# Attention logits turned by DMA instead of TensorE, with a new order of loads and new costs in the planner

## The chip, the core and the metric

The kernel runs on one core of a Trainium2 chip. A core has five engines, each with its own queue of instructions that it works off in order: TensorE (PE; its weight loads are PEld), VectorE (DVE), ScalarE (ACT), GpSimd (POOL) and SyncE (SP). SP computes nothing here; it issues DMAs, which ACT and POOL do as well. The metric is the device time in microseconds (us) of one execution; lower is better. A profile is taken of one execution; its span runs from the first to the last instruction of the program.

## The reference

A layer norm feeds two branches whose outputs are added to the input. Branch A is a dilated sliding-window attention: each position looks at W=8 earlier positions, 2 apart, with 32 heads of 20 elements. Branch B is a gated unit without an activation.

```
xn = layernorm(x)                        # x: 2048 x 640, bfloat16
q, k, v = xn @ wqkv                      # 32 heads of 20
logits[h,s,w] = q[h,s] . k[h, s - 2w] / sqrt(20)     # -1e9 where s - 2w < 0
attn = softmax(logits, over w)           # 8 values
o[h,s] = sum_w attn[h,s,w] * v[h, s - 2w]
out = x + o @ wo + ((xn @ w_gate) * (xn @ w_up)) @ w_down     # inner width 1536
```

## The kernel before

The 2048 rows are 16 tiles of 128 (numbered 0 to 15), in four chunks of four tiles (chunk 0 to 3). PE turns the normed rows (`x`) of the first eight tiles into `xnT`; a transposing DMA on SP does it for the other eight. From `xnT` PE makes q, k (line 338), v (line 362) and the gate and up values (line 515). The loop over chunks is `attention(c)`, `glu(c)`, then `down` for the four tiles of the chunk, in between which the layer norm of chunk c+2 is done, then q, k and v of chunk c+2.

**Attention.** For each window place i of 8, DVE multiplies q by the shifted k (`pw`, line 394; five buffers). PE sums each head's 20 products with a matrix of ones, four places at a time (line 404): a logits group. There are two groups in a chunk, numbered here 0 to 7 over the kernel. ACT copies each group from PSUM to `L` in f32 (line 413); in chunk 0 DVE then adds the mask to the first 14 columns (line 415). PE transposes `L` back, four 128x128 blocks for each half chunk (two tiles), into PSUM (`pS`, line 426). DVE takes the maximum over the window with a reduce (line 434) and subtracts it (436), ACT takes the exponential (441), DVE sums with a reduce (448), inverts (449) and multiplies (451). These last three are called the norm here.

The v rows are stored to a DRAM scratch `vD`, and SP loads each tile's eight shifted copies back into one of three `v8` buffers: "value t" is that load for tile t, 1,280 KB (line 461). DVE multiplies it by the weights (line 476) and adds the eight copies in three steps (485, 489, 491); a transposing DMA on SP turns the result into `oT` (line 498).

**glu(c)** is 24 matmul groups of five (12 gate and up pairs). ACT copies each from PSUM (line 520; three gate and two up buffers) and DVE multiplies each pair into one of the twelve `hT` (line 531). **down** accumulates twelve `hT` products (553) and five `oT` products (556) for each half of a tile, and DVE adds the rows of x to it (`xr`, line 562). For the first tile of a chunk both halves first run ten `hT` products and the five `oT` products; the last two `hT` products of both halves come after, here the closing matmuls.

**PSUM.** Six banks (`ps`) go round in turn for all of PE's main work, one holds the logits, one the transposed logits.

**What sets the order.** The program is a list of `Step`s, each with an engine, a cost, an occupancy and its dependencies. `Plan.order` runs a list schedule with them and emits the instructions in that order; nothing is reordered later, and the waits between engines follow from the tiles. Steps marked urgent go ahead of others that are ready. `floor` is the earliest end that the planner assumes for a load. PE's main work is one fixed chain; what the planner decides is between which of its pieces the logits groups fall, and how DVE's, ACT's and SP's steps interleave. On SP the early loads are chained by hand: the first x tile, the weights wv, wq, wk, gate and up, then value 0, 1, 2, then w_down (wd) and wo.

Of the kernel before, what the change touches and what calls it, by code (L numbers as in the profile page):

```python
# [9 lines left out]
ACT = mybir.ActivationFunctionType  # L10
# [4 lines left out]
class Step:  # L15


    __slots__ = ("eng", "cost", "deps", "fn", "late", "succ", "idx", "start", "end", "left", "occ", "urgent", "after", "floor")

    def __init__(self, eng, cost, fn, deps, occ=None, after=()):  # L20
        self.eng, self.cost, self.fn = eng, cost, fn
        self.after = [d for d in after if d is not None]
        self.deps = [d for d in deps if d is not None] + self.after
        self.occ = cost if occ is None else occ
        self.succ = []
        self.urgent = False
        self.floor = 0.0


class Plan:  # L30


    LAG = {"PE": 0.25, "ACT": 0.22, "DVE": 0.12, "POOL": 0.2, "SP": 0.1}
# [10 lines left out]
    def order(self):  # L44
# [15 lines left out]
        while True:  # L60
# [16 lines left out]
            for t in s.succ:  # L77
                t.left -= 1
                if t.left == 0:
                    at = max(  # L80
                        d.start + d.occ if d in t.after else d.end + (0.0 if d.eng == t.eng else self.LAG[d.eng])
# [8 lines left out]
def kernel(  # L90
# [49 lines left out]
    ident_f = const.tile([P, P], F32, name="ident_f")  # L140
# [40 lines left out]
    WL["g"].floor, WL["u"].floor = 19.0, 25.0  # L181
# [7 lines left out]

    def consts_f():  # L190
        make_identity(nc, ident_f[:])
# [28 lines left out]
    C0 = add("POOL", 1.5, consts0)  # L220
    CE = add("POOL", 1.4, consts_e, [C0])
    CM = add("POOL", 0.8, consts_m, [C0])
    CF = add("POOL", 0.7, consts_f, [C0])
# [39 lines left out]
    def ln(t):  # L263
        a = add("DVE", 0.45, ln_stats(t, 0), [X[t], GL.get(t - 3)])
        a = add("DVE", 0.45, ln_stats(t, 1), [a])
        a = GL[t] = add("DVE", 0.36, ln_aggr(t), [a])
        b = add("POOL", 0.6, ln_rstd(t), [a])
        XT[t] = add("DVE", 0.45, ln_apply(t), [b])
# [4 lines left out]
    def pe_main(cost, fn, deps=(), banks=1):  # L273
# [5 lines left out]
        main = add("PE", cost, fn, [main, *waits, *deps])  # L279
# [5 lines left out]
    def transposes(t):  # L285
# [19 lines left out]
        if t < XDMA:  # L305
            a = pe_main(0.29, pe, [XT[t]])
            TT[t] = add("ACT", 0.7, ev, [a])
            ring.append(TT[t])
        else:
            a = TT[t] = add("SP", 3.5, dma, [XT[t], GP.get(c - 2)], occ=1.0)  # L310
# [19 lines left out]
    def qk(c, lo, n, rs=(0, 1)):  # L330
        for r in rs:
            for j in range(KT):
# [14 lines left out]
                a = pe_main(KT * (n / 2400 + 0.003), pe,  # L347
                            [WK if r else WQ, *[TT[c * CH + t] for t in range(lo // P, (lo + n) // P)], LASTPW.get(c - 2)])
                e = add("ACT", 0.16 + n / 1200, ev, [a, HALOCP[c]])
# [5 lines left out]
    def vproj(t):  # L355
        c, q = divmod(t, CH)
        evs = []
        for n in range(2):
# [15 lines left out]
            e = add("ACT", 0.6, ev, [a, VS.get(t - 3), CZ])  # L374
# [6 lines left out]
        VS[t] = add("POOL", 2.2, st, evs, occ=0.5)  # L381


    PW, LL, LE, SS, DD, AA, O16, OE, V8, DT = {}, {}, {}, {}, {}, {}, {}, {}, {}, {}

    def prodlog(c):
        for g in range(2):
            n = 2 * c + g
            for j in range(4):
# [7 lines left out]
                PW[m] = add("DVE", 1.48, mul, [*Q[c], *Kk[c], LL.get((m - 5) // 4) if m >= 5 else None])  # L397
            LASTPW[c] = PW[m]

            def lg(g=g):  # L400
                l = new(("lps", c, g), [P, 512], F32, "pl", 1, psum)
# [6 lines left out]
            LL[n] = add("PE", 1.25, lg, [*[PW[8 * c + 4 * g + j] for j in range(4)], LE.get(n - 1), CE])  # L408
            LL[n].urgent = True

            def ev(g=g):
                L = new(("L", c, g), [P, CS], F32, "L", 2)
                nc.scalar.copy(L[:], T["lps", c, g][:])
                if c == 0:
                    nc.vector.tensor_tensor(L[:, 0:HALO], L[:, 0:HALO], negm[:, g, :], ALU.add)

            LE[n] = add("ACT", 0.7, ev, [LL[n], SS.get(2 * c - 1), CM])

    def softmax(c, hf):
        n = 2 * c + hf  # L420

        def tr():
            ps = new(("atp", n), [P, 2, 2, P], F32, "pS", 1, psum)
            for t in range(2):
                for g in range(2):
                    nc.tensor.transpose(ps[:, t, g, :], T["L", c, g][:, (2 * hf + t) * P : (2 * hf + t + 1) * P], ident_f[:])  # L426

        SS[n] = add("PE", 0.45, tr, [LE[2 * c], LE[2 * c + 1], DD.get(n - 1), CF])
        SS[n].urgent = True

        def mx():
            L4 = T["atp", n][:].rearrange("p t g (w h) -> p t (g w) h", w=4, h=H)
            m = sb.tile([P, 2, H], F32, name="m", tag="m", bufs=2)
            nc.vector.reduce_max(m[:], L4.rearrange("p t w h -> p t h w"), AX.X)
            d = new(("d", n), [P, 2, W, H], F32, "d", 2)
            nc.vector.tensor_tensor(d[:], L4, m[:, :, None, :].to_broadcast([P, 2, W, H]), ALU.subtract)

        DD[n] = add("DVE", 1.4, mx, [SS[n], AA.get(n - 2)])
# [4 lines left out]
        e = add("ACT", 0.65, ex, [DD[n]])  # L443

        def nrm():
            d = T["d", n]
            s = sb.tile([P, 2, H], F32, name="s", tag="s", bufs=2)
            nc.vector.reduce_sum(s[:], d[:].rearrange("p t w h -> p t h w"), AX.X)
            nc.vector.reciprocal(s[:], s[:])
            a = new(("a", n), [P, 2, W, H], BF, "a", 2)  # L450
            nc.vector.tensor_tensor(a[:], d[:], s[:, :, None, :].to_broadcast([P, 2, W, H]), ALU.mult)

        AA[n] = add("DVE", 2.2, nrm, [e, O16.get(2 * n - 3)])

    def load_v8(t):
# [6 lines left out]
        V8[t] = add("SP", 6.0, fn, [VS[t], VS.get(t - 1), O16.get(t - 3), CZ], occ=0.5, after=[WL["u"]])  # L462
        if t < 3:
            V8[t].floor = 30.0 + 4.3 * t
        if t == 2:
            WL["d"] = add("SP", 8, wload(wd, B_w_down), after=[V8[2]], occ=0.5)
            WL["o"] = add("SP", 8, wo_load, after=[WL["d"]], occ=2.0)
            WL["d"].floor, WL["o"].floor = 46.0, 49.0
# [200 lines left out]
```

## Time and profile before

| | |
|---|---|
| median of three runs (lowest, highest) | 274.73 us (272.54, 275.71) |
| the profiled execution: its time | 273.97 us |
| its span | 272.3 us |
| TensorE clock granted, mean | 0.994 |
| share of DMA engines' time, queue of SP | 43.7% |

The profile's page gives each engine's busy time, the chain of work that ended last (followed back from the last instruction to whatever released it), the costliest groups of instructions, and the DMA issues with the time until they landed. Groups read: line, engine, operation, output<-inputs, shapes, xcount | busy us in all, mean ns of one | idle time of the engine just before them, and what ended it. A timeline row reads: start us, duration us, engine, line, operation, tiles. In the rows of the chain the columns are start us, duration us, what.

The profiled execution lies within the three runs, 0.76 us under their median.

### The profile page before, as it was taken

How to read it: one execution, taken by the hardware profiler on the slowest of the kernel's cores; microseconds unless marked ns; L12 is line 12 of the kernel's file. 1: busy time of each engine (PE TensorE's matmuls, PEld its weight loads, DVE VectorE, ACT ScalarE, POOL GpSimd, SP SyncE). 2: the span in 40 equal slices, each digit the busy share in tenths (PEclk: the TensorE clock that was granted, in tenths of full speed). 3: DMA queues.
4: the chain of work that ended last, by engine and by line, in shares of the span. 5: the costliest groups of instructions: out<-in, count | busy, mean ns of one | idle time of the engine just before them, and what ended most of it. 6: DMA issues, size and time to landing. Idle time of an engine off the chain costs nothing.

```text
span 272.3 us, 4126 instructions
## 1 busy us (share of the span) xinstructions
PE 263.3 (97%) x1608; PEld 146.1 (54%) x1626; DVE 216.5 (80%) x302; ACT 108.0 (40%) x197; POOL 39.7 (15%) x83
## 2 busy tenths in 40 slices
PE   5899999999999999999999999999999999999994
PEld 1554447444476555544456664644447774445773
DVE  4644999999998968999998389999974999991221
ACT  2467656555500155465520025755551005554000
POOL 6431006400000242300001201200000212000000
PEclk9799999999999999999999999999999999999999
DMA  7999999452759830557795213697500156111001
GB/s 230 382 403 382 367 365 250 156 173 63 225 108 275 270 98 26 134 182 217 224 269 64 72 51 88 236 280 220 191 0 2 48 149 202 38 24 26 24 24 48
DMA packets 43156, 44.85 MB, mean 165 GB/s; under 512 B 17587, under 2 KB 40385, under 8 KB 43137
## 3 DMA queue, kind: packets, MB, share of 16 engines
q1 hardware_dynamic: 39168, 35.07, 43.7%
q0 software_dynamic: 2240, 7.56, 8.3%
q10 hardware_dynamic: 1728, 1.97, 2.1%
q8 instruction: 12, 0.20, 0.3%
q14 instruction: 8, 0.06, 0.1%
HBM read 35.39 MB, written 5.26 MB: 149 GB/s over the span
## 4 chain that ended last, share of the span: by engine, by line
PE 92%; DMA 4%; DVE 2%; issue 1%; ACT 0%
PE ps L515 38%; PE ps L553 19%; PE ps L338 13%; PE ps L362 8%; PE ps L556 8%; DMA x<-in_A_x_dram 4%; PE pl L404 4%; PE pS L426 1%; DVE st L238 1%; PE ps L295 1%; DVE x L257 0%; ACT xnT L299 0%; DVE mv L244 0%; DVE xr L562 0%; DVE ve L246 0%
## 5 line engine op out<-in xcount | busy, mean ns | idle before, releaser
L515 PE MATMUL ps<-xnT,wu 128*128 128x512 bf16 x240 | 59.6, 379 | 0.0
L515 PE MATMUL ps<-xnT,wg 128*128 128x512 bf16 x228 | 59.0, 379 | 0.6
L553 PE MATMUL ps<-wd,hT 128*128 128x320 bf16 x384 | 57.4, 299 | 0.0
L394 DVE TENSOR_TENSOR pw<-q,k 128x2560 bf16<-128x2560 bf16 x32 | 46.6, 1484 | 0.8 <-PE pl L404 0.7
L553 PEld LDWEIGHTS <-hT 128*128 128x128 bf16 x384 | 37.2, 98 | 16.2 <-issue 1.7
L476 DVE TENSOR_TENSOR v<-v,a 128x5120 bf16<-128x5120 bf16 x16 | 45.1, 2819 | 0.1
L515 PEld LDWEIGHTS <-wu 128*128 128x128 bf16 x240 | 23.5, 98 | 28.3
L515 PEld LDWEIGHTS <-wg 128*128 128x128 bf16 x240 | 23.4, 98 | 27.9 <-issue 0.4
L520 ACT CAST us<-ps 128x512 bf16<-128x512 f32 x48 | 28.1, 586 | 23.9 <-PE ps L515 20.3
L520 ACT CAST gs<-ps 128x512 bf16<-128x512 f32 x48 | 28.1, 586 | 20.7 <-PE ps L515 20.7
L562 DVE TENSOR_TENSOR xr<-ps,xr 128x320 bf16<-128x320 f32 x32 | 15.2, 487 | 20.7 <-PE ps L556 17.3
L584 POOL DMA_DIRECT2D out_dram<-xr x14 | 7.6, 542 | 139.7 <-DVE xr L562 139.3
L556 PE MATMUL ps<-wo,oT 128*128 128x320 bf16 x160 | 27.0, 299 | 0.0
L531 DVE TENSOR_TENSOR hT<-gs,us 128x512 bf16<-128x512 bf16 x48 | 19.7, 420 | 8.9 <-ACT us L520 8.8
L362 PE MATMUL ps<-wv,xnT 128*128 128x320 bf16 x160 | 24.2, 308 | 0.3 <-ACT xnT L299 0.3
L485 DVE TENSOR_TENSOR v<-v 128x2560 bf16<-128x2560 bf16 x16 | 23.7, 1484 | 0.1
L338 PE MATMUL ps<-xnT,wq 128*128 128x512 bf16 x96 | 22.4, 379 | 0.2
L238 DVE BATCH_NORM_STATS2 st<-x 128x6 f32<-128x320 bf16 x32 | 14.0, 482 | 10.3 <-DMA x<-in_A_x_dram 10.1
L338 PE MATMUL ps<-xnT,wk 128*128 128x512 bf16 x98 | 22.0, 379 | 0.1
L362 PEld LDWEIGHTS <-xnT 128*128 128x128 bf16 x160 | 15.8, 100 | 7.5 <-ACT xnT L299 0.5
L345 ACT CAST q<-ps 128x512 bf16<-128x512 f32 x20 | 11.7, 585 | 18.3 <-PE ps L338 17.3
L556 PEld LDWEIGHTS <-oT 128*128 128x128 bf16 x160 | 15.7, 98 | 6.1
(51 smaller groups left out, 191.6 us busy)
## 6 DMA issues: line engine op xcount, KB each, us to landing
v<-vD SPq DMA_DIRECT2D x16, 1280.0 KB, 7.3
vD<-v_t POOLq DMA_DIRECT2D x16, 160.0 KB, 2.7
xr<-in_A_x_dram POOLq DMA_DIRECT2D x16, 160.0 KB, 2.6
out_dram<-xr POOLq DMA_DIRECT2D x14, 160.0 KB, 2.1
x<-in_A_x_dram ACTq DMA_DIRECT2D x12, 160.0 KB, 6.1
wg<-in_B_w_gate_dram SPq DMA_DIRECT2D x1, 1920.0 KB, 14.7
wu<-in_B_w_up_dram SPq DMA_DIRECT2D x1, 1920.0 KB, 18.8
wd<-in_B_w_down_dram SPq DMA_DIRECT2D x1, 1920.0 KB, 19.9
```

Of the source, the lines that this page charges most:

```text
L238: nc.vector.bn_stats(T["st", t][:, g, :], T["x", t][:, g * NS : (g + 1) * NS])
L338: nc.tensor.matmul(ps[:, 0:n], lhsT=(wk if r else wq)[:, i, j * P : (j + 1) * P], rhs=T["xnT", c][:, i, lo : lo + n], start=(i == 0), stop ...
L362: nc.tensor.matmul(ps[:, 0:NS], lhsT=T["xnT", c][:, i, q * P : (q + 1) * P], rhs=wv[:, i, n * NS : (n + 1) * NS], start=(i == 0), stop=(i ...
L394: nc.vector.tensor_tensor(p[:], T["q", c][:], T["k", c][:, :, DIL * i : DIL * i + CS], ALU.mult)
L476: nc.vector.tensor_tensor(v[:].rearrange("p w (j h) -> p w j h", j=Dh, h=H), v[:].rearrange("p w (j h) -> p w j h", j=Dh, h=H), T["a", n][ ...
L485: nc.vector.tensor_tensor(v[:, 0:4, :], v[:, 0:4, :], v[:, 4:8, :], ALU.add)
L515: nc.tensor.matmul(ps[:], lhsT=(wu if r else wg)[:, i, f * P : (f + 1) * P], rhs=T["xnT", c][:, i, :], start=(i == 0), stop=(i == KT - 1))
L520: nc.scalar.copy(s[:], T[key][:])
L531: nc.vector.tensor_tensor(h[:], T["gs", c, f][:], T["us", c, f][:], ALU.mult)
L553: nc.tensor.matmul(ps[:, 0:NS], lhsT=T["hT", c, f][:, q * P : (q + 1) * P], rhs=wd[:, f, sl], start=(f == 0), stop=(f == FT - 1 and not wo ...
L556: nc.tensor.matmul(ps[:, 0:NS], lhsT=T["oT", t][:, g, :], rhs=wo[:, g, sl], start=False, stop=(g == KT - 1 and f1 == FT))
L562: nc.vector.tensor_tensor(T["xr", t][:, sl], T["psD", t, n][:, 0:NS], T["xr", t][:, sl], ALU.add)
```

## The change

Logits. The copy on ACT now writes `L` in bf16; the mask of chunk 0 is added by DVE in PSUM before that copy. A transposing DMA on SP turns each group into `LT`, one bf16 buffer for the whole chunk; a chunk's softmax needs both groups. The eight sets of f32 transposes on PE are gone, and with them the f32 identity that POOL made. The freed PSUM bank gives the logits two. The two reduces become three pairwise steps each over the window (8 to 4 to 2 to 1): bf16 for the maximum, f32 for the sum.

SP's early loads now go value 0, wd, logits 0, value 1, logits 1, wo, value 2.

The planner has new costs: for steps of DVE, PE and ACT that follow each other on one engine only the occupancy counts, the lag between engines is 0.06, logits groups are held back by a margin of 0.5 after their products, and the floors of loads are new.

The diff, without most of the lines that only change a cost:

```diff
-    LAG = {"PE": 0.25, "ACT": 0.22, "DVE": 0.12, "POOL": 0.2, "SP": 0.1}
+    LAG = 0.06
+    INORDER = ("DVE", "PE", "ACT")
...
-                        d.start + d.occ if d in t.after else d.end + (0.0 if d.eng == t.eng else self.LAG[d.eng])
+                        d.start + d.occ if d in t.after else (d.start + d.occ if d.eng == t.eng and d.eng in self.INORDER else d.end + (0.0 if d.eng == t.eng else self.LAG) + t.margin)
...
-    WL["g"].floor, WL["u"].floor = 19.0, 25.0
+    WV.floor, WQ.floor, WK.floor = 6.4, 13.6, 13.7
+    WL["g"].floor, WL["u"].floor = 18.0, 25.2
...
-    CF = add("POOL", 0.7, consts_f, [C0])
...
-                l = new(("lps", c, g), [P, 512], F32, "pl", 1, psum)
+                l = new(("lps", c, g), [P, 512], F32, "pl", 2, psum)
...
-            LL[n] = add("PE", 1.25, lg, [*[PW[8 * c + 4 * g + j] for j in range(4)], LE.get(n - 1), CE])
+            LL[n] = add("PE", 1.28, lg, [*[PW[8 * c + 4 * g + j] for j in range(4)], LE.get(n - 2), CE], occ=1.195)
             LL[n].urgent = True
+            LL[n].margin = 0.5
 
             def ev(g=g):
-                L = new(("L", c, g), [P, CS], F32, "L", 2)
+                L = new(("L", c, g), [P, CS], BF, "L", 2)
+                if c == 0:
+                    ps = T["lps", c, g]
+                    nc.vector.tensor_tensor(ps[:, 0:HALO], ps[:, 0:HALO], negm[:, g, :], ALU.add)
                 nc.scalar.copy(L[:], T["lps", c, g][:])
-                if c == 0:
-                    nc.vector.tensor_tensor(L[:, 0:HALO], L[:, 0:HALO], negm[:, g, :], ALU.add)
...
+            def tr(g=g):
+                if g == 0:
+                    new(("LT", c), [P, CH, W, H], BF, "LT", 1)
+                out = T["LT", c][:].rearrange("p t (g w) h -> p t g (w h)", g=2)[:, :, g, :]
+                nc.sync.dma_start_transpose(out=out, in_=T["L", c, g][:])
+
+            early = [SPLAST[0]] if c == 0 else []
+            SS[n] = SPLAST[0] = add("SP", 3.5, tr, [LE[n], DD.get(2 * c - 1), DD.get(2 * c - 2)], occ=1.25, after=early)
+            if c == 0 and g == 0:
+                load_v8(1)
+                SPLAST[0] = V8[1]
...
-        def tr():
-            ps = new(("atp", n), [P, 2, 2, P], F32, "pS", 1, psum)
-            for t in range(2):
-                for g in range(2):
-                    nc.tensor.transpose(ps[:, t, g, :], T["L", c, g][:, (2 * hf + t) * P : (2 * hf + t + 1) * P], ident_f[:])
...
-            nc.vector.reduce_max(m[:], L4.rearrange("p t w h -> p t h w"), AX.X)
+            nc.vector.tensor_tensor(m[:], L4[:, :, 0:4, :], L4[:, :, 4:8, :], ALU.max)
+            nc.vector.tensor_tensor(m[:, :, 0:2, :], m[:, :, 0:2, :], m[:, :, 2:4, :], ALU.max)
+            nc.vector.tensor_tensor(m[:, :, 0:1, :], m[:, :, 0:1, :], m[:, :, 1:2, :], ALU.max)
...
-            nc.vector.reduce_sum(s[:], d[:].rearrange("p t w h -> p t h w"), AX.X)
-            nc.vector.reciprocal(s[:], s[:])
+            nc.vector.tensor_tensor(s[:], d[:, :, 0:4, :], d[:, :, 4:8, :], ALU.add)
+            nc.vector.tensor_tensor(s[:, :, 0:2, :], s[:, :, 0:2, :], s[:, :, 2:4, :], ALU.add)
+            nc.vector.tensor_tensor(s[:, :, 0:1, :], s[:, :, 0:1, :], s[:, :, 1:2, :], ALU.add)
+            nc.vector.reciprocal(s[:, :, 0, :], s[:, :, 0, :])
...
+    def load_down():
+        WL["d"] = SPLAST[0] = add("SP", 8, wload(wd, B_w_down), after=[SPLAST[0]], occ=0.5)
+        WL["d"].floor = 36.0
+
+    def load_out():
+        WL["o"] = SPLAST[0] = add("SP", 8, wo_load, after=[SPLAST[0]], occ=5.0)
+        WL["o"].floor = 49.0
...
     def attention(c):
+        if c == 0:
+            SPLAST[0] = WL["u"]
+            load_v8(0)
+            load_down()
         prodlog(c)
+        if c == 0:
+            load_out()
+            load_v8(2)
```

In the changed program, as built, PE's main chain is the same. The logits groups move along it: group 2 from behind tile 2 of down(0) to behind tile 1, group 3 from behind the first q group of chunk 2 into the middle of tile 3 of down(0), group 4 from behind the first products of tile 0 of down(1) to behind the eleventh pair of glu(1), group 5 to where group 4 was, groups 6 and 7 from behind 18 and 24 matmul groups of glu(2) to behind 11 and 16. On DVE, three products of chunk 1 stand ahead of the first softmax (before: one), and both halves' maxima stand together ahead of the first norm. In chunk 1 the order on SP is `oT` of tile 3, values 5 and 6, the x tiles 13, 14 and 15, logits 2 and 3; before it was value 5, x tiles 13 and 14, `oT` of tile 3, value 6, x tile 15.

## The prediction

> **What bounds the kernel now.** First the busy times, then the chain of waits, then the groups that the change touches.
>
> ```profile
> PE 263.3 (97%) x1608; PEld 146.1 (54%) x1626; DVE 216.5 (80%) x302; ACT 108.0 (40%) x197; POOL 39.7 (15%) x83
> ...
> PE 92%; DMA 4%; DVE 2%; issue 1%; ACT 0%
> PE ps L515 38%; PE ps L553 19%; PE ps L338 13%; PE ps L362 8%; PE ps L556 8%; DMA x<-in_A_x_dram 4%; PE pl L404 4%; PE pS L426 1%; DVE st L238 1%; PE ps L295 1%; DVE x L257 0%; ACT xnT L299 0%; DVE mv L244 0%; DVE xr L562 0%; DVE ve L246 0%
> ```
>
> PE is the bound, and the transposes to be removed (L426) are on its chain. But DVE's 80% is no even 80%: it is over 95% busy from 40 to 80 us, so it is the second bound there. The groups, kept apart by shape:
>
> ```profile
> L531 DVE TENSOR_TENSOR hT<-gs,us 128x512 bf16<-128x512 bf16 x48 | 19.7, 420 | 8.9 <-ACT us L520 8.8
> L448 DVE TENSOR_REDUCE s<-d 128x64 f32<-128x512 f32 x8 | 8.3, 1032 | 0.7 <-ACT d L441 0.7
> L451 DVE TENSOR_TENSOR a<-d,s 128x512 bf16<-128x512 f32 x8 | 5.5, 692 | 0.3
> L436 DVE TENSOR_TENSOR d<-pS,m 128x512 f32<-128x512 f32 x8 | 5.5, 692 | 0.3
> L434 DVE TENSOR_REDUCE m<-pS 128x64 f32<-128x512 f32 x8 | 5.5, 686 | 3.6 <-PE pS L426 3.6
> L426 PE MATMUL pS<-ident_f,L 128*128 128x128 f32 x32 | 4.8, 272 | 0.0
> L449 DVE RECIPROCAL s<-s 128x64 f32<-128x64 f32 x8 | 4.4, 553 | 0.3
> ```
>
> Then the timelines of PE and DVE, the chain between 73 and 90 us, SP's issues, and two stretches of the traffic (the last number is GB/s):
>
> ```profile
> 41.91 1.53 PE L362 MATMUL ps<-wv,xnT 128*128 128x320 bf16 x10
> 43.28 0.60 PE L426 MATMUL pS<-ident_f,L 128*128 128x128 f32 x4
> 43.71 2.88 PE L362 MATMUL ps<-wv,xnT 128*128 128x320 bf16 x20
> ```
> ```profile
> 49.21 2.82 DVE L476 TENSOR_TENSOR v<-v,a 128x5120 bf16<-128x5120 bf16 x1
> ...
> 75.86 0.42 DVE L531 TENSOR_TENSOR hT<-gs,us 128x512 bf16<-128x512 bf16 x1
> ```
> ```profile
> 78.36 2.17 PE ps L553 x16
> ```
> ```profile
> 79.62 0.53 SPq L461 DMA_DIRECT2D v<-vD  x1
> ...
> 83.59 4.36 SPq L159 DMA_DIRECT2D x<-in_A_x_dram  x1
> ```
> ```profile
> 86.50:88.50 2.00, 2.00 (x21) 1.19 (x22) 1.98 (x3) 0.00 (x0) 0.04 (x1) 1.00 1.42 131
> 89.00:93.00 4.00, 4.00 (x36) 2.71 (x29) 3.93 (x7) 0.58 (x1) 0.55 (x1) 1.00 1.10 366
> ```
> ```profile
> 94.50 2.44 DVE L238 BATCH_NORM_STATS2 st<-x 128x6 f32<-128x320 bf16 x6
> ```
>
> DVE finishes the twelfth hT of chunk 0 at 76.3; PE's closing matmuls, which start at 78.36, need it at 78.5. DVE has 2.2 us to spare.
>
> **Off PE.** Ten value matmuls take 1.36 on the chain, but the next twenty start 1.80 after the first ten (41.91 to 43.71): one set of four transposes costs 0.44. Eight sets: 3.5 us, each on the path.
>
> **Start.** Tile 0 is normed ahead of the second half of tile 2's statistics, one piece of 0.4, so PE starts 0.4 sooner. Group 1 needs the eighth product, though. The products start about 0.3 sooner, with the k copies and x tile 9; then three pieces of statistics stand before the mask instead of two (+0.4). So the eighth still ends at 40.4, and group 1 starts at 40.5 instead of 40.78. Gain 0.3 (0, if x tile 9 is no earlier, to 0.8).
>
> **DVE's new steps.** Pairwise bf16 work has rows at 512 (420 ns) and 2560 elements (1484): 0.15 + 0.52 per thousand, so the maxima over 256, 128 and 64 take 0.29, 0.22, 0.19; the subtraction stays 0.69. In f32 (692 at 512, same fixed part) the sums take 0.42, 0.29, 0.22. A step that needs the one before it starts 0.035 after it; an independent one 0.08 before its end. So the maximum and subtraction take 1.41, the norm 2.23. Before, start to start, 1.33 (58.69 to 60.02) and 2.26 (62.39 to 64.65). Nothing gained; the order is what matters.
>
> **Chunk 0: hT 12 (a new wait).** From 40.4 DVE has two statistics 0.80, three aggregates 0.90, a product 1.42, the mask 0.10, three rows normed 1.08, two more products 2.83: 47.5. The transposed logits must be there: mask done 43.7, copy 0.585, so issued at 44.35; the transposing DMA of five blocks lands in 2.6, here four, 47.0. Hidden, by 0.5. Then two maxima 2.82, norm 2.23: 52.6 (before: 49.21). Up to hT 12: eleven hT 3.69, four value multiplies 10.96, three first adds 4.34, three second adds 3.78, the second norm 2.23: 77.6, done 78.05. The same rows over the old order give 75.5 against 75.86, 0.4 of it waits. PE needs it at 78.5 - 0.28 - 0.88 = 77.35. Stall 0.7. Bounds: 0, if dependent steps overlap like the others; 2.4, if that DMA takes the slowest `xnT` transpose's 4.3 (+1.2) and the maxima run at the f32 price (+0.5). Group 2 then finds its products ready within 0.1: both engines are late by the same amount.
>
> A rule speaks against moving this work. The Trainium skill, VectorE: DVE Perf Modes, section The three transpose paths, gives 390 ns for a 128x128 transpose on TensorE and 1309 ns for one by DMA, and its rules say to use TensorE if PSUM will do. The trace is cheaper: five blocks land in 2.6. By the page's price, an estimate, four blocks take 5.2 us, the logits land at 49.6 and the stall grows by 2.1; the sum below would be +1.0 instead of -1.1.
>
> **Chunk 1: group 4 (the other new wait).** It moves forward into glu(1), to where PE arrives at 112.72 - 1.76 - 0.28 + 0.7 = 111.4, plus eleven pairs at 2.137 (24 groups took 112.72 to 138.36): 134.9. Its fourth product is DVE's last thing after all of chunk 1's attention. That starts after x tile 15: before, it landed at 94.54 and DVE's six statistics began then. Now SP gets to value 5 later: chunk 0's last result at 80.8, its transpose, 82.1. Value 5, value 6 and three x tiles, 3.1 MB, are queued ahead of tile 15's landing and of logits 2 and 3. At best one value lands in its shortest 5.4 and the other 1.8 MB moves at 350 GB/s (338 and 366 in the two clean stretches of this traffic), 5.1: 92.6. At worst the 14.9 of before (79.62 to 94.54): 97.0. With the median landing of 7.3, 94.5; I take 94.0. Then statistics 1.6, an eviction 0.4, aggregates 0.9, POOL's last two rstd 1.5, norming and eviction 0.8: 99.2. (Logits 3 are issued at 93.7; 2.6 or 4.3 both hide.) Two maxima and the norm 5.05; four value multiplies 10.96, first adds 5.75, second adds 5.04, norm 2.23, nine hT 3.0, four products 5.67: 136.9. Stall 2.0, from 0 (92.6) to 5.0 (97.0), a microsecond for each that tile 15 is late. Chunk 2's products, by the same walk, are about 1 us ahead of groups 6 and 7.
>
> **At nothing.** POOL's identity (0.63) was off the path. On SP logits 0 waits at the head for ACT's copy (near 37) with value 1 behind it: value 1 goes out at 38 instead of 20, lands at its median of 7.3 near 46 and is used at 57. Logits 1 hold back wo and value 2 until 46; four wo pieces of 0.6 and the landing put value 2 near 56, used at 69, and wo before it, used at 75. wd is moved ahead of value 1: up to it SP's bytes are fewer than those that had landed by 38.9 before (values 0 to 2), and it is used at 73. Each would cost what it came late; the shortest cover is value 1's 11 us. The copies of group 1 wait for the mask, with the v copies behind them on ACT, which start at 44.4 instead of about 42.5: 1.9, covered by six PSUM banks, 4.1 us of value matmuls. ACT's exponential then waits ahead of the gate copies until near 51; PE has banks until 53.5.
>
> **The sum.** -3.5 - 0.3 + 0.7 + 2.0 = -1.1. The profiled time of 273.97 becomes 272.9; from the median of 274.73 it is 273.6. I say 273.2.
>
> **Rivals.** *Neither wait appears*: PE's order is unchanged otherwise, so -3.8, 270.2 to 270.9. For: both stalls hang on margins of 1 to 2 us in sums of 40. Against: DVE's 95%. *Slower than before*: values 5 and 6 drain slowly ahead of x tile 15. Before, between 86.5 and 88.5 the traffic fell to 131 GB/s while a transpose was between two values, and that can repeat. The stall at group 4 must exceed 3.1, so tile 15 must land after 95.1; at 97 it is +1.9, 276.2, and past 98 the exponentials that wait at the head of ACT's queue hold the q copies as well, 278. *The transposes cost PE nothing*, as idle time elsewhere would take their place: 0, but PE has only 4.5 us of idle in pieces over 0.15, all before 27 us. Little.
>
> **The numbers.** No stall of note 0.33; the forecast's case 0.45, 271.8 to 274.6; slower than before 0.22. Runs of before spread over 1.2%, so about 1% is what can be told from no change. Faster by over 1% needs the stalls under 1.1 together: the first case, 0.33. Slower by over 1% needs them over 6.5: 0.14. Within 1%: 0.53. The range leaves a tenth at each end: 269.9 (no stall, start gains 0.8) to 276.6. The forecast's own range is 271.8 to 274.6.
>
> **What would show it.** No L426 rows; PE 3.5 us less busy. Step one: an idle piece on PE before the closing matmuls at 77 to 79, ended by hT. Step two: idle before group 4 near 135, ended by pw, with x tile 15 landing near 94. The maximum and norm at 1.4 and 2.2. Transposes of `L` landing in under 3 us in chunk 0. The prediction fails if PE shows no such pieces, if it waits elsewhere (groups 0 to 3, `xr` evictions after the statistics), or if new DVE steps cost half again as much.

## The result, and the profile after

The changed kernel takes 276.65 us (median of 20 runs, 274.01 to 278.55) beside 274.60 (20 runs, 272.54 to 276.20) of the kernel before. The ratio is 1.0066, with a 95% interval of 1.0042 to 1.0089: slower by 0.7%, where 273.2 was forecast. Here and below the ratio is formed from executions within 1.5% of their kernel's fastest, so it can differ a little from that of the medians.

Its profile fell on the fastest of the 20 executions: 274.01 us, with a span of 272.3, as before the change, and at a granted clock of 1.000. Busy times and chain on its page:

```profile
PE 261.7 (96%) x1594; PEld 142.3 (52%) x1594; DVE 215.3 (79%) x334; ACT 105.8 (39%) x197; POOL 39.0 (14%) x81
...
PE 52%; DVE 35%; DMA 7%; issue 2%; POOL 1%; SPq 1%; ACT 1%; DVEq 0%; POOLq 0%
```

PE was 92% of the chain and is 52% now; DVE went from 2% to 35%. The transposes are off PE, and in their place stand stretches in which PE waits for DVE. PE's timeline (start us, duration us, engine, line, tiles; in brackets the idle time ahead and what ended it) shows them:

```profile
8.29 1.53 PE L360 MATMUL ps<-wv,xnT 128*128 128x320 bf16 x10
...
76.75 1.53 PE L568 MATMUL ps<-wd,hT 128*128 128x320 bf16 x10 [0.99 <-DVE hT L546]
...
99.61 1.67 PE L336 MATMUL ps<-xnT,wk 128*128 128x512 bf16 x7 [0.43 <-DVE xr L577]
...
134.27 0.39 PE L403 MATMUL pl<-pw,Ek 128*32 128x512 bf16 x2
136.01 0.38 PE L403 MATMUL pl<-pw,Ek 128*32 128x512 bf16 x1 [1.34 <-DVE pw L393]
137.75 1.24 PE L403 MATMUL pl<-pw,Ek 128*32 128x512 bf16 x17 [1.36 <-DVE pw L393]
```

Only the first row is good news: ten value matmuls at the start take 1.53, where they took 2.55 before:

```profile
9.00 2.55 PE L362 MATMUL ps<-wv,xnT 128*128 128x320 bf16 x10 [0.25 <-ACT xnT L299]
```

The others are waits: the closing matmuls of chunk 0, the first k group of chunk 2, and group 4, where PE has two of the four products, then waits for the third and again for the fourth.

What each wait costs is read from where PE's stages begin (first matmul of each, from the same timelines, in us; the last column is the end of PE's work):

| | glu(0) | down(0) | q of chunk 2 | glu(1) | down(1) | q of chunk 3 | glu(2) | down(2) | end |
|---|---|---|---|---|---|---|---|---|---|
| before | 48.23 | 74.12 | 93.90 | 112.29 | 138.19 | 160.14 | 176.36 | 204.85 | 268.74 |
| after | 45.48 | 71.38 | 93.62 | 110.44 | 141.09 | 160.86 | 177.08 | 205.76 | 268.77 |
| after, second profile | 48.37 | 74.27 | 96.51 | 113.14 | 145.23 | 165.00 | 181.23 | 209.72 | 272.74 |

A logits group takes 1.20 and a set of transposes 0.44. Between before and after, with these put where they moved: up to glu(0) -2.75 (two sets 0.88, the start 1.87); down(0) +2.46 (group 3 moved in 1.20, the wait at hT 12 1.26); from q of chunk 2 to glu(1) -1.57 (group 3 moved out 1.20, two sets 0.88, the wait at k 0.5); glu(1) +4.75 (group 4 in 1.20, its wait 3.55); down(1) -2.18 (a group and two sets); down(2) -0.89 (two sets); the rest +0.2. The sum is 0.03. The waits cost more than the idle pieces say (1.26 for a piece of 0.99, 3.55 for 2.70): the last matmul ahead of a wait is shown to its end, 0.38 us for 512 columns, while in an unbroken row the next one starts 0.216 after it. As remainders of this account, 1.26 and 3.55 also hold about 0.1 each that isn't assigned.

So the profiled pair is level only since this execution of the changed kernel started 1.9 us faster. Against that stand -3.5 of transposes and +5.3 of waits, +1.8 together; the medians differ by 2.05. PE's busy time is no measure of the transposes: it fell by 1.6 (263.3 to 261.7).

DVE's new steps, by shape (x count | busy, mean ns | idle before):

```profile
L454 DVE TENSOR_TENSOR s<-d 128x256 f32<-128x256 f32 x8 | 3.3, 418 | 0.0
L455 DVE TENSOR_TENSOR s<-s 128x128 f32<-128x128 f32 x8 | 2.3, 292 | 0.3
L438 DVE TENSOR_TENSOR m<-LT 128x256 bf16<-128x256 bf16 x8 | 2.3, 286 | 0.9 <-DMA LT<-L 0.9
L456 DVE TENSOR_TENSOR s<-s 128x64 f32<-128x64 f32 x8 | 1.8, 225 | 0.3
L439 DVE TENSOR_TENSOR m<-m 128x128 bf16<-128x128 bf16 x8 | 1.8, 224 | 0.3
L440 DVE TENSOR_TENSOR m<-m 128x64 bf16<-128x64 bf16 x8 | 1.5, 192 | 0.3
```

They cost what was worked out from the old rows (0.29, 0.22, 0.19 and 0.42, 0.29, 0.22). The transposing DMAs of chunk 0 landed 2.5 and 2.4 us after their issue, the second at 45.07.

### The profile page after: what moved, and what is told of

Read it like the earlier page. It is cut to its first block, busy times and chain, and to the rows that moved or that the text cites. A ratio compares the mean times of both kernels' runs of the same rounds, so it can differ in the third digit from the quotient of the medians.

```text
span 272.3 us, 4128 instructions
## 1 busy us (share of the span) xinstructions
PE 261.7 (96%) x1594; PEld 142.3 (52%) x1594; DVE 215.3 (79%) x334; ACT 105.8 (39%) x197; POOL 39.0 (14%) x81
## 4 chain that ended last, share of the span: by engine, by line
PE 52%; DVE 35%; DMA 7%; issue 2%; POOL 1%; SPq 1%; ACT 1%; DVEq 0%; POOLq 0%
PE ps L530 20%; PE ps L568 14%; DVE v L491 8%; DMA x<-in_A_x_dram 7%; DVE pw L393 7%; PE ps L571 6%; PE ps L336 6%; DVE v L500 4%; PE ps L360 4%; DVE st L236 3%; DVE v L504 2%; DVE hT L546 2%; PE pl L403 2%; DVE o L506 1%; POOL rstd L250 1%
## 5 line engine op out<-in xcount | busy, mean ns | idle before, releaser
L530 PE MATMUL ps<-xnT,wg 128*128 128x512 bf16 x240 | 59.7, 379 | 0.0
L360 PE MATMUL ps<-wv,xnT 128*128 128x320 bf16 x160 | 22.9, 299 | 0.0
```

The costliest lines, as they stand in the source:

```text
L360: nc.tensor.matmul(ps[:, 0:NS], lhsT=T["xnT", c][:, i, q * P : (q + 1) * P], rhs=wv[:, i, n * NS : (n + 1) * NS], start=(i == 0), stop=(i ...
L530: nc.tensor.matmul(ps[:], lhsT=(wu if r else wg)[:, i, f * P : (f + 1) * P], rhs=T["xnT", c][:, i, :], start=(i == 0), stop=(i == KT - 1))
```

## The experiments

Times are medians; the ratio is to runs of the kernel before taken on the same chip.

### The same kernel again

> The changed kernel unaltered, for a second profile. Its first profile is the only one of 20 runs at a granted clock of 1.000 (span 272.3 us); the others show 0.994 and spans near 274.9. Theory A (waits on DVE plus a start at a reduced clock): at 0.994 the trace shows PE slower or idle in the first 15 us, by about 2.6 us in all, as the kernel before had it (ten value matmuls in 2.55 there against 1.53), and from 40 us on the same pieces of idle PE as the first profile: 1.0 ended by hT near 77, 0.4 ended by xr near 100, 2.7 at logits group 4 near 136. Theory B (the transfers vary): the start is the same, and the 2.6 us stand at group 4 or at a wait on a DMA. Time 276.6 for both.

276.03 us (273.71 to 278.34, 10 runs), ratio 1.002 (0.9985 to 1.0056). The profile fell on an execution of 277.99 us, among the slowest of the ten. PE's timeline in it:

```profile
8.96 2.85 PE L360 MATMUL ps<-wv,xnT 128*128 128x320 bf16 x10
...
138.71 0.38 PE L403 MATMUL pl<-pw,Ek 128*32 128x512 bf16 x1 [1.34 <-DVE pw L393]
140.44 2.29 PE L403 MATMUL pl<-pw,Ek 128*32 128x512 bf16 x17 [1.36 <-DVE pw L393]
```

The waits at group 4 are the same to 0.01 us, so theory B's varying transfers fall. Two other things differ. At the start the same ten matmuls take 2.85 instead of 1.53, and all of PE's work up to 13.7 runs at half speed: 320 columns every 267 ns instead of 136. glu(0) starts 2.9 later; 0.4 of it stands already ahead of the first transposes (at 7.46 instead of 7.05). And behind group 4's wait, 17 matmuls take 2.29 instead of 1.24: half speed again, to 143.5, which makes glu(1) longer by 1.44. Theory A named the start and not the second stretch. Of the 30 executions of this kernel in both sets 3 show a granted clock of 1.000 (273.71 to 274.36); the other 27, at 0.994 or less, have a median of 276.7. That gap of 2.7 us is what the first profile doesn't show. A clock of 0.994 says little of where it arises: the one stretch granted half speed in this profile, 3.4 us from 140.1, lowers the mean over 276 us by just that much, and the slow start isn't in it.

### Where do the waits come from: the planner or the logits?

Group 4 alone put back:

```diff
-            LL[n].margin = 0.5
+            LL[n].margin = 3.5 if n == 4 else 0.5
```

> Logits group 4 alone is given a margin of 3.5 us, so that it stands behind the first products of tile 0 of down(1), as in the kernel before; groups 5 to 7 move a little later with it. Theory A (the place that the planner gave group 4 makes PE wait): the 2.7 us go, 276.65 becomes 274.0, level with the kernel before. Theory B (DVE is late by as much whatever PE does): the wait comes back at the closing matmuls of chunk 1 or at group 5, and the time stays at 276.6. Theory C (the loss is in DMA traffic or the clock): no change either, but without a new wait.

274.21 us (272.52 to 274.78, 10 runs), ratio 0.9975 (0.9949 to 1.0001). Theory A's number, but not quite its mechanism. The wait at group 4 is gone, and a piece of 1.76 stands at the next thing that needs DVE, as theory B said, since DVE's products now stand ahead of the tenth hT:

```profile
140.10 0.31 PE L568 MATMUL ps<-wd,hT 128*128 128x320 bf16 x1 [1.76 <-DVE hT L546]
```

The logits part alone, in the planner and the loads of before (line of the copy and the transposing DMA as in the change, PSUM banks too, nothing else):

```diff
+                nc.sync.dma_start_transpose(out=out, in_=T["L", c, g][:])
...
+            SS[n] = add("SP", 3.5, tr, [LE[n], DD.get(2 * c - 1), DD.get(2 * c - 2)], occ=1.25)
```

> The logits part alone (bf16 copy, mask in PSUM, transposing DMA, two logits banks, pairwise maxima and sums), with the planner, the costs and the order of loads of the kernel before. Group 4 lands behind the eleventh pair of glu(1) here too; groups 2 and 3 stand later than in the changed kernel. Theory A: 3.5 us of transposes off PE, no wait at hT 12 of chunk 0, a wait at group 4 of 0 to 3: 271.1 to 274.1. Theory C (the transposing DMA is what costs): 276 or more, with PE idle behind a chain that shows the landing of LT.

274.58 us (273.53 to 277.36, 10 runs), ratio 1.0009 (0.9972 to 1.0045): between the theories. No wait on the landing of `LT` shows on PE. There is no wait at group 4, but it doesn't stand where it was expected either: it comes at 146.5, behind the closing matmuls of tile 0 of down(1), so this run says nothing of the place in glu(1). PE waits 0.63 at the tenth hT of chunk 0, 0.18 at group 2, 0.28 for an `oT`, and 0.70 at the value matmuls of chunk 2, behind ACT's copies of k. The 3.5 us don't come out in this order either.

The planner and the loads alone, with the old logits (f32 copy, transposes on PE in one bank, reduces):

```diff
+            SS[n] = add("PE", 0.45, tr, [LE[2 * c], LE[2 * c + 1], DD.get(n - 1), CF])
-            SS[n] = SPLAST[0] = add("SP", 3.5, tr, [LE[n], DD.get(2 * c - 1), DD.get(2 * c - 2)], occ=1.25, after=early)
```

> The planner, its costs, the margin and the order of loads of the changed kernel, with the logits as before (f32 copy, transposes on PE in one bank, reduces). Theory A (waits made by the new places of the groups): the eight sets of transposes are back, 3.5, and the waits stay: about 280, from 278 to 281. Theory C (the DMA path of the logits is what costs): at the kernel before's 274.6, within 1.

277.99 us (277.42 to 279.65, 4 runs), ratio 1.0132 (1.0085 to 1.0180). The time is at theory A's lower end; the places aren't its. No wait at hT 12 and none at group 4, which stands half a pair earlier here; instead 2.5 us ahead of transposes, ended by DVE's subtraction or mask, and a start at half speed to 13.7. So the planner's costs put PE and DVE too close together with either path, and it depends on the path where that shows.

### Is the half speed caused by the wait?

Eight matmuls into group 4's own bank, ahead of it:

```diff
+                if c == 2 and g == 0:
+                    for _ in range(8):
+                        nc.tensor.matmul(l[:], lhsT=ident[:], rhs=T["xnT", 1][:, 0, :], start=True, stop=True)
```

> The changed kernel, with eight matmuls of 512 columns put on PE right ahead of logits group 4, into the bank that the group then overwrites. PE has 2.7 us of idle there, and the eight take 1.73 at 0.216, so they use only idle time. In the second profile of the changed kernel 19 matmuls after this idle time ran at about half speed (steps of 427 ns for 512 columns instead of 216), at a granted clock of 0.994 in the mean; in the first profile none did, at 1.000. Theory A1 (the idle time trips PE's clock, which costs a further 1.6 in most runs): with the idle time filled the half-speed stretch goes, the clock is 1.000 in most runs, and 276.3 becomes about 274.7. Theory A2 (the half speed comes from elsewhere, such as power): the time stays at 276 to 276.7 and 0.994 stays.

275.83 us (274.36 to 277.06, 10 runs), ratio 1.0064 (1.0026 to 1.0102). The clock is 0.998 or more in 6 of 10 runs instead of 3 of 30, but the time hardly moved, and that the idle time makes the difference isn't shown. These runs are from another chip, on which the longer warm-up of the next section gave 1.000 in 7 of 10 with all of the 2.7 us left; and with group 4 put back, so with no idle time there and 1.76 us behind it, 8 of 10 read 0.997 or less. Of the 2.7 us a wait of 1.35 is left behind the eight. What the half-speed stretch costs in the median isn't settled by this: 1.4 in the one execution that shows it.

### The start

```diff
-        for _ in range(10):
+        for _ in range(16):
```

> The changed kernel, with 16 instead of 10 matmuls in the warm-up of PE. In its first profile PE was at full speed from the first transposes at 7.05 on; in the second at half speed until 13.6, and glu(0) began 2.9 us later. Theory S (how long PE is busy before 7 us decides whether it starts at half speed): the extra six matmuls at 427 ns keep PE busy to about 8.2 and move the first transposes back by up to 1.2, but no run is at half speed past 9; the median falls by 1 (275.0 to 275.7) and the spread narrows. Rival (the speed at the start is drawn from something else): the median rises by about 1, to 277, and the spread stays at 4.

275.61 us (274.43 to 277.53, 10 runs), ratio 1.0039 (1.0001 to 1.0077). PE was at full speed from its eighth warm-up matmul on, and 7 of 10 runs show a clock of 1.000. The spread is 3.1 instead of 4.5. The median is as expected, but by the ratios (1.0066 and 1.002 for the changed kernel) a gain isn't clear of noise. Its first transposes came at 8.52, not for the warm-up, which ended at 6.6, but for DVE, whose queue waited for x tile 2 (landed at 7.60). That wait is in both kernels, so tiles 0 and 1 were normed first:

```diff
-        a = add("DVE", 0.48, ln_stats(t, 0), [X[t], GL.get(t - 3)], occ=0.395)
+        a = add("DVE", 0.48, ln_stats(t, 0), [X[t], GL.get(t - 3)], occ=0.395, after=[XT[1]] if 2 <= t < 5 else [])
```

> The changed kernel, with the statistics of x tiles 2 to 4 put behind the norming of tiles 0 and 1 in the planner's list. In the traces so far PE's first transposes come between 6.94 and 8.52, because DVE's queue has tile 2's first statistics ahead of that norming, and tile 2 lands between 5.7 and 7.6. Theory S: the first transposes come at 6.6 to 6.8 in every run, PE's idle time ahead of them shrinks to under 0.9, half speed at the start becomes rarer, and the median falls by 0.5 to 1.5 (275.0 to 275.8). Rival (tile 2's own transposes are the bound of the start): no change, 276.3.

275.89 us (273.94 to 277.49, 10 runs), ratio 1.0023 (0.9997 to 1.0050). First transposes at 6.98; by the medians the gain is 0.1 to 0.8, just short of what was expected, by the ratios it isn't told from nothing, and 9 of 10 runs still show 0.994 or 0.993.

> The kernel before, with the statistics of x tiles 2 to 4 behind the norming of tiles 0 and 1, as in the run of the changed kernel with that order: tells what a better kernel owes to the start rather than to the logits. Theory S: 0.3 to 1 us faster, 273.6 to 274.3. Rival: the same as the kernel before.

273.83 us (272.44 to 275.36, 10 runs), ratio 0.9948 (0.9924 to 0.9973): 0.8 to 1.4 us, by the base taken, a little more than expected. What is gained at the start is no merit of either logits path.

### Why is DVE late?

Products of chunk 1 behind the last hT of chunk 0:

```diff
-..., occ=1.395)
+..., occ=1.395, after=[HT[c - 1, FT - 1]] if c == 1 else [])
```

> The changed kernel, with the products of chunk 1 put behind the last hT of chunk 0 in the planner's list (one planner dependency); groups 2 to 5 move back by up to two pieces. Theory A: the 1.0 ended by hT 12 near 77 goes, as three products of 1.42 leave DVE's path ahead of it; group 4 stands where it did before the change (behind the second half of down(1)'s first tile), so its wait goes or shrinks below 1, with the half-speed stretch: 276.3 becomes 272 to 274. Theory B (the work put back returns as a wait): PE waits at groups 2 or 3 or at the closing matmuls of chunk 1 by 2 us or more, and the time stays above 275.

277.62 us (275.67 to 278.62, 4 runs), ratio 1.0106 (1.0024 to 1.0189). Theory B. No wait is left at hT 12 and none at group 4; PE waits for the products put back, at group 3, and runs at half speed from 100.6 to 106.4 behind that:

```profile
PE pl L404 <- DVE pw L393: 4.4, 4, 1.8
```

(us in total, times, longest.) Next, x tiles 13 to 15 loaded by POOL instead of SP:

```diff
-            e = "ACT" if t < XDMA else "SP"
+            e = "ACT" if t < XDMA else "POOL"
```

> The changed kernel, with the loads of x tiles 13, 14 and 15 issued by POOL instead of SP; everything else, the order on PE and DVE too, is unchanged. In the profile of the changed kernel those loads land at 93.3 to 94.2, behind values 5 and 6 on SP, and DVE idles 3.4 us for them ahead of chunk 1's softmax. Theory A (group 4's wait is that landing, one us per us, as the prediction had it): the tiles land near 84, DVE's idle 3.4 goes, the 2.7 at group 4 and the 0.4 at the first k group go, and the half-speed stretch with them: 276.3 becomes 272 (271.3 to 273). Theory B (DVE is short of time in any case, or the values are slowed by as much): the wait stays above 1.5, 275 or more.

279.91 us (279.03 to 280.95, 4 runs), ratio 1.0200 (1.0122 to 1.0278). The tiles landed at 83.0 to 90.5, and DVE waited 6.7 us for POOL's rstd instead. The wait at group 4 and the time are theory B's, but not its cause; the first k group waits 3.5. So the loads went back to SP, ahead of values 5 and 6:

```diff
-        order = [SPLAST[0]] if t < CH - 1 else []
+        order = [SPLAST[0]] if t < CH - 1 else [X[13], X[14], X[15]] if t in (5, 6) else []
```

> The changed kernel, with values 5 and 6 put behind x tiles 13, 14 and 15 on SP; nothing else is moved, and POOL's queue is as it was (in the run with the loads on POOL the rstd steps stood behind loads that waited for stores, and DVE idled 6.7 us for them). Theory A (group 4's wait comes from the landing of x tile 15, one us per us): the tiles land at 85 to 88, DVE's idle 3.4 us ahead of the statistics goes, and with it the 2.7 at group 4, the 0.4 at the first k group and the half-speed stretch behind group 4: 276.3 becomes 272.2 (271.5 to 273.2). Theory B (values 5 and 6 are then late by as much): DVE waits for value 5 near 105, the wait at group 4 stays above 1.5, and the time above 275.

277.30 us (274.20 to 278.72, 10 runs), ratio 1.0065 (1.0034 to 1.0097): no gain, though the tiles landed at 85.5 to 88.4 instead of 93.3 to 94.2. DVE's waits between 84 and 106, in the changed kernel and then in this one:

```profile
DVE st L236 <- DMA x<-in_A_x_dram: 3.4, 1, 3.4
```
```profile
DVE x L255 <- POOL rstd L250: 5.2, 1, 5.2
```

The reason stands in POOL's timeline of this run:

```profile
93.37 0.54 POOL L555 DMA_DIRECT2D xr<-in_A_x_dram  x1 [6.79 <-DMA out_dram<-xr]
94.25 0.55 POOL L599 DMA_DIRECT2D out_dram<-xr  x1 [0.34 <-DVE xr L577]
94.81 0.57 POOL L250 TENSOR_TENSOR rstd<-ve,mhalf 128x1 f32<-128x1 f32 x1
99.84 0.58 POOL L555 DMA_DIRECT2D xr<-in_A_x_dram  x1 [4.47 <-DMA out_dram<-xr]
100.45 1.60 POOL L250 TENSOR_TENSOR rstd<-ve,mhalf 128x1 f32<-128x1 f32 x3
```

Three rstd of 0.5 us stand behind an xr load. That load waits for a store of results to free its buffer, and the store shares the traffic with values 5 and 6 (the two stores issued while these were under way took 6.8 and 5.3 us to land, the one before and the one after 2.8 and 3.2). What it loads isn't needed before down(1), at 141. In the changed kernel the same load was let go at 96.47, and rstd followed at 97.07, when DVE had just got there. Two limbs of one wait, then. The run that had been planned beside it, with the last hT of chunk 0 ahead of the multiply as well,

```diff
+    m, h = steps.index(MUL[3]), steps.index(HT[0, FT - 1])
+    steps.insert(h, steps.pop(m))
```

> The changed kernel with three steps of order undone or mended: values 5 and 6 behind the x tiles (as above), tiles 0 and 1 normed ahead of tile 2's statistics (as above), and the last hT of chunk 0 ahead of the fourth value multiply on DVE, which in the profile stood ahead of it by 2.8 us while its inputs had been there. Theory A: no wait of note is left on PE; 276.3 less 2.7, 0.4, 1.0, the half-speed stretch of 1.1 and about 0.7 at the start: 270.4 (269.5 to 271.6), below the kernel before by over 1%. Theory B (DVE short of time whatever the order): the waits come back at later groups, 273 or more.

gave 275.78 us (274.82 to 279.49, 12 runs), ratio 1.0042 (1.0014 to 1.0071). The time is theory B's. The wait at hT 12 is gone, but 1.36 is left at group 4, 0.7 at group 2, and there are 3.0 us at the first k group: POOL's limb once more. Now both limbs:

```diff
+    for t in range(4, 8):
+        a, b = steps.index(XR[t]), steps.index(RS[15])
+        if a < b:
+            steps.insert(b, steps.pop(a))
```

> The changed kernel with values 5 and 6 behind x tiles 13 to 15 on SP, and with the four rstd steps of that layer norm ahead of the xr loads of tiles 4 to 7 on POOL (those loads wait for the stores of the last results, which share the traffic of values 5 and 6; they are needed only after 140). Theory A' (two limbs of the same wait: x tiles behind the values on SP, rstd behind stores on POOL; each alone only uncovers the other): DVE's idle time between 84 and 104 falls below 1, the wait at group 4 below 0.5, the wait at the first k group goes, and no half speed behind it: 276.3 becomes 272.2 (271.5 to 273.2). Theory B (DVE is short of time in any case): the wait at group 4 stays above 1.5 and the time at 275 or more.

273.70 us (271.63 to 276.46, 10 runs), ratio 0.9952 (0.9923 to 0.9982): 2.6 below the changed kernel (276.3; by the ratios 1.9 to 3.1), where 4 were expected. The rstd steps alone, with the loads left as they were, weren't tried. The wait for rstd and the one at k are gone; what DVE still waits for is the logits' own transpose, behind the values on the same queue:

```profile
DVE m L438 <- DMA LT<-L: 1.4, 1, 1.4
```

At group 4 a piece of 1.36 remains, and between 99.4 and 137 DVE is busy for 36.8 of 37.6 us. There theory B has a part: where the planner put group 4, DVE is late even when nothing holds it.

### The versions with several amendments

> As the run before, and also the last hT of chunk 0 ahead of the fourth value multiply, and tiles 0 and 1 normed ahead of tile 2's statistics. Theory A': every wait of note on PE after the start is gone; 276.3 less 2.7, 0.4, 1.0, 1.1 of half speed, and 0.4 at the start: 270.7 (269.8 to 272), below the kernel before by over 1%. Theory B: 273.5 or more.

273.70 us (270.72 to 275.91, 12 runs), ratio 0.9935 (0.9898 to 0.9973). The waits left are small (0.3 at group 4, 0.7 at group 2, 0.6 at group 0), but the start of the profiled execution was slow, with 1.4 us of waiting for wv. The median misses the forecast by 3.0 and lies where theory B had it, though the profile doesn't show waits of that size.

> The changed kernel with group 4's margin of 3.5 (276.3 became 274.2 with that alone), the last hT of chunk 0 ahead of the fourth value multiply, and tiles 0 and 1 normed ahead of tile 2's statistics; loads and POOL's queue as they are. Theory A: the 1.0 near 77 goes as well, about 0.4 at the start; the 1.8 at the closing matmuls of chunk 1 stays: 272.8 (272.2 to 273.6). Theory B (a wait taken away ahead only lengthens the one behind, as DVE's chain through x tile 15 sets the time of chunk 1): the 1.0 is added to the wait in chunk 1, and the time stays at 273.8 to 274.2.

274.18 us (272.95 to 275.88, 10 runs), ratio 0.9980 (0.9952 to 1.0008): theory B, the same as with the margin alone. Where the traffic isn't touched, the 1.0 saved in chunk 0 comes back as 1.4 at k and 0.7 at group 2, and the 1.8 in chunk 1 stays.

> All five: group 4's margin, values 5 and 6 behind the x tiles, rstd ahead of the xr loads, the last hT of chunk 0 ahead of the value multiply, tiles 0 and 1 normed first. If the run without the margin has no wait left at group 4, this one is the same within 0.5; if one is left there, this one is faster by it: 270.2 to 271.5.

270.91 us (270.19 to 276.36, 6 runs), ratio 0.9866 (0.9826 to 0.9905). Neither the kernel before nor the changed one is as fast. How much of that is the margin isn't shown: the medians with and without it differ by 2.8, but 2.0 of the 2.3 us between the two profiles arise ahead of glu(0) (47.73 against 49.77), where the margin does nothing.

> The version with all five amendments once more, beside its twin with the transposes on PE. Its first six runs gave 270.9 (270.2 to 276.4). Theory A: 270.9, within 0.6.

270.71 us (269.83 to 273.18, 6 runs), ratio 0.9855 (0.9821 to 0.9888). PE's waits in it, all of them:

```profile
PE ps L227 <- POOL ident masks.py:199: 1.4, 1, 1.4
PE ps L293 <- DVE x L255: 1.0, 1, 1.0
PE pl L404 <- DVE pw L394: 0.7, 1, 0.7
PE ps L360 <- ACT xnT L297: 0.3, 1, 0.3
```

Three of the four belong to the start; 0.7 is group 2. Beside it, the same amendments with the logits as before:

> The same five amendments on the kernel that has the changed planner and loads but the logits as before: f32 copy, eight sets of transposes on PE, reduces. Group 4's margin is 5.5 here, so that the group stands at the same place, behind the first products of tile 0 of down(1). Theory A (the transposes cost PE 0.44 a set wherever they stand, and that comes out in full once no other wait is there): 270.9 + 3.5 = 274.4, from 273.8 to 275. Rival (idle time on PE would have covered them): within 1 of 270.9.

275.16 us (274.12 to 277.69, 12 runs), ratio 1.0022 (0.9998 to 1.0047). (In this kernel the value multiply of tile 3 stands behind the first of its adds, so half of tile 3's terms get the weights of other places, and it doesn't compute the reference; the instructions are the same.) The difference to its twin is 4.4, by the spans of the two profiles 4.0. By stage, down(1) and glu(2) are longer by 0.88 each: two sets of 0.44, with no wait beside them. The other four sets come with waits of PE for DVE,

```profile
PE pS L434 <- DVE d L444: 1.0, 2, 0.7
...
PE pS L434 <- DVE L L421: 0.4, 1, 0.4
```

1.4 in all against 0.7 at group 2 in the twin, and the start of this execution was 0.8 faster than that of its twin. So half of the sets are seen to cost what they were put at; for all eight 3.5 fits, but the other half can't be parted from the waits that come with them.

## Why the prediction was wrong

**Off PE, -3.5: right.** down(2), which no wait touches, lost 0.89 with two sets; the last pair of runs shows 0.88 for two sets twice, and a difference of 4.4 with all eight and the waits that come with them.

**DVE's new steps, nothing gained: right,** to 0.01 us a step. Only the first of a chunk's two maxima with its subtraction took 1.53 from start to start instead of 1.41; the second took 1.42.

**Transposing DMA: right in chunk 0** (landed 2.43 after its issue, put at 2.6; at 45.07 and not at 47.0, as the issue came at 42.65 and not at 44.35). The Trainium skill's 1309 ns for a 128x128 block (VectorE: DVE Perf Modes, section The three transpose paths) would have made, as an estimate, 5.2 us of four blocks; with SP's queue free they took 2.4 to 2.5. In chunk 1 the pair behind the values took 9.8 and 4.6, which x tile 15 and POOL hid in the changed kernel.

**hT 12, +0.7: the place was right, the term too small.** It cost 1.26. My walk ended on DVE at 78.05 with the last hT behind all four multiplies; it ended at 76.7, as the walk began 1.4 sooner (first maximum at 46.10, put at 47.5), but PE was there 1.7 sooner, at 75.6 and not at 77.35. DVE's timeline shows what the sum hid:

```profile
73.53 2.82 DVE L491 TENSOR_TENSOR v<-v,a 128x5120 bf16<-128x5120 bf16 x1
76.27 0.42 DVE L546 TENSOR_TENSOR hT<-gs,us 128x512 bf16<-128x512 bf16 x1
```

The last copy that this hT needs ended on ACT at 72.7. Not DVE's load but the order of these two rows made the wait, and turning them round removed it. No run shows that the time fell by it: with the loads and POOL's queue left as they were, waits came back elsewhere.

**The first k group: missed, 0.5.** I named `xr` evictions behind the statistics as a way to fail and gave them no term.

**Group 4, +2.0: the step that failed most.** It cost 3.55. Tile 15 landed at 94.22 against the 94.0 that I took, and the fourth product ended at 137.7 against 136.9. PE came at 134.27, not at 134.9. So 0.6 of the missing 1.5 is PE's earlier start, by luck, and 0.8 is DVE's: 0.3 up to the first maximum (99.47, put at 99.2), 0.5 in the walk from there (38.2, put at 37.7). The price of "a microsecond for each that tile 15 is late" fell outright: 5.8 us earlier gained nothing (the run with the x tiles first), because POOL's rstd was as late for the same traffic. It was in my walk as "POOL's last two rstd 1.5", without what is queued ahead of them on POOL. With both limbs moved 1.36 was left; the margin alone sent 1.76 on to the next hT; with all five amendments group 4 has no wait.

**Start, -0.3: wrong as a kind of term.** The two profiles of the same kernel differ by 2.9 there. I took the start of one execution as a property of the kernel.

**The sum.** My 272.9 for the profiled execution compares with 274.01: waits 2.6 larger than the 2.7 put down, the start 1.6 better by luck. From there to the median of 276.65 are 2.6 more. The second profile shows what they are made of in one execution, a later start (2.9, some 2.5 of it half speed) and half speed behind group 4 (1.44). How they mix over many runs isn't shown, only that 27 of 30 have a lower clock. The rival "slower than before" had the right sign and a wrong mechanism: it needed tile 15 after 95.1, and tile 15 was in time.

## What to carry to other kernels

Taking work off the bounding engine pays only as far as the second engine follows: here DVE was over 95% busy beside it, and a planner that closed the gaps between the two turned 3.5 us of gain into 5.3 us of waits. Before a wait is priced by one transfer, look for a second queue that waits for the same traffic, small steps behind a blocked load above all; moving the loads alone gained nothing here. And where an order is planned, ask of each wait whether the engine is out of time or only has two ready steps in the wrong order: the second kind is mended by turning the two round, though here no run shows what that alone gains.

## What was not expected of the hardware

PE runs its first matmuls at half speed (512 columns every 427 ns, 216 later). When the half speed of the start ends differs from execution to execution: at 10.2 us in the run with group 4 put back, at 13.7 in the second profile of the changed kernel. The Trainium skill describes this (TensorE: Matmul & The Clock Gate, section What's actually happening): a free-running window of about 3.4 us decides, so the moment varies from run to run. The runs agree. In the kernel before, full speed was granted for 3.4 us and taken back for as long (stretch, us, PE busy (matmuls), granted clock, DMA share, GB/s):

```profile
4.29:7.70 3.41, 0.99 (x6) 1.00 1.01 360
7.71:11.12 3.41, 3.16 (x19) 0.50 1.06 375
```

Between the two profiles of the changed kernel this is worth some 2.5 us of a 272 us kernel. The granted clock doesn't always tell of it. The same stretch in the second profile and in the kernel before:

```profile
7.00:14.00 7.00, 6.47 (x33) 1.00 1.06 382
```
```profile
7.00:14.00 7.00, 6.17 (x46) 0.76 1.06 383
```

The first has nearly every matmul at half speed and reads 1.00; the second ran faster and reads 0.76, as full speed had been granted at 4.3 and was taken back at 7.7. It is durations that must be compared.

Half speed also came back in the middle of the kernel: for 3.4 us behind waits of 2.7 us in two pieces (group 4, second profile), of 2.0 and of 3.0 (the first k group with the x tiles first, and with three amendments), for 6.8 behind 4.2 in three pieces (the products behind the last hT). That section of the skill speaks of about one idle window, 3.4. Here less was enough, though not each time: the first profile of the changed kernel and those of the two runs of it on the start have the same 2.7 and no such stretch. Nor was more always enough; with the x tiles on POOL the matmuls behind a longer wait ran at full speed, nine in 2.10 us:

```profile
104.23 2.10 PE L336 MATMUL ps<-xnT,wk 128*128 128x512 bf16 x9 [3.54 <-DVE xr L577]
```

What decides between these cases isn't shown.
